# A four-layer attention and GLU kernel: the order of the first chunk's set-up, a shared scratch tile, masks by one minimum, and a planner with ranks

## The chip, the cores and the metric

The kernel runs on one core of one Trainium2 chip. A core has a matrix engine (TensorE, PE), a vector engine (VectorE, DVE), a scalar engine (ScalarE, ACT), a general engine (GpSimd, POOL) and a sync engine (SyncE, SP) that issues DMA transfers here. Each engine works through its own list of instructions in order and waits on semaphores that other engines or transfers raise. The metric is the device time of one execution, in microseconds; lower is better.

## The reference

Four layers run over x of shape [1, 2048, 576]: attention, GLU, attention, GLU, all with the same two sets of weights. Each layer adds its result to its input after a layer norm without scale or offset:

```python
x = x + _A_ref(_layernorm(x), A_wqkv, A_wo)
x = x + _B_ref(_layernorm(x), B_w_gate, B_w_up, B_w_down)
...
```

Attention has 32 heads of 18 values. A position attends to itself and to the seven positions 2, 4, ..., 14 steps before it; positions before the start are masked:

```python
idx = pos[:, None] - off[None, :]        # off = 0, 2, ..., 14
logits = jnp.where(idx >= 0, einsum("bhsd,bhswd->bhsw", q, kg) * scale, -1e9)
o = jnp.einsum("bhsw,bhswd->bhsd", softmax(logits), vg)
...  # then o @ wo
```

The GLU computes ((x @ w_gate) * (x @ w_up)) @ w_down with 4608 hidden values and no activation function. Inputs and output are bf16.

## The kernel before

**Tiling.** The 2048 positions are cut into chunks of 256; the first four chunks of the first attention layer have 128. `seq` lists 18 chunks, numbered j from 0: six of the first attention layer (0 to 3 with 128 positions), then four of the second over the same first 1024 positions, then four and four over the other 1024. For each chunk the kernel does attention and then the GLU (`attention(j, ...)`, `glu(j, ...)`). All weights stay in SBUF except w_down, of which 288 KB pieces (`wd`, seven buffers) are loaded again for each chunk.

**Attention of a chunk.** `head` (L356) does the layer norm: statistics on DVE, two small steps on ACT for 1/sigma (`rstd`), one on DVE (`nmr`), the normalisation on ACT (`xn`), a transpose on PE for the first five chunks (L395, by transposing DMA later), and the copy out of PSUM on ACT (L400). `project` (L446, matmuls in L456) computes q, k and v with heads along partitions; the weights are copied once into another column order for that (`wqkv` from `wraw`, L310 DVE, L312 POOL, L314 ACT). DVE multiplies q by two shifted k's at a time (four products, L554); PE sums them over the values of a head with a 0/1 matrix (`Esel`, L569); softmax runs on DVE and ACT (L590 to L602); PE spreads the weights over the partitions (L612); DVE multiplies them with the eight shifted v's (L642), PE (chunk 0, L646 and L647) or DVE (L656) adds these up; PE multiplies by wo (L669), in four pieces for 256 positions and two for 128, and DVE adds the residual (L675). A second `head` prepares the input of the GLU, `xnT_B`.

**GLU of a chunk.** Three phases, each of gate and up matmuls (L720; L731 for the last 64 rows of the contraction), a copy of gate on ACT (L742), a product on DVE (L743), the down matmuls (L759, L760) and an addition to x on DVE (L772).

**The order.** Nothing is ordered by hand. Every step is an `op` with an engine, an estimated cost, the keys it reads and writes, a priority and a `margin` (a time by which it is planned later than its inputs allow). `Plan.run` (L74) simulates the engines with these estimates: it takes the op that can start first, by (time, priority, index), and emits its instructions in that order. Its one exception: ops marked `due` (the GLU's L742 and L743) may take the place of another op of their engine:

```python
if not o.due and o.eng in urgent and urgent[o.eng][0][0] < best[0][0] + o.cost - SLACK[o.eng]:
    best = urgent[o.eng]
```

What an engine does in hardware is this order; the times are those of the hardware. PE, DVE and ACT so hold the work of several chunks mixed: the GLU of one chunk, the attention of the next ones.

**The start.** SP issues, in this order: x of the first 128 positions, the raw wqkv weights in six transfers (four of 128 rows with all 1728 columns, and twice the last 64 rows), x of three more chunks' positions, x for chunk 4, wo (six), then the GLU's weights in six slices with the first `wd` pieces between them. Each transfer uses one of eight semaphores in turn, so that it is issued once the eighth transfer before it has landed. In chunk 0 (`fast`) the projection runs over the five row blocks of the weights as they arrive, and each row block's matmuls wait for q, k and v columns alike. `wraw` lives in a pool of its own that is given back (`swap`) when all copies are done; the product buffers, `Lt` and `ab` are taken from the same place after that. Masks of chunk 0 are seven memsets on the logits in PSUM (L590).

Of the kernel before, what the change touches and what calls it, by code (L numbers as in the profile page):

```python
# [7 lines left out]
FP32 = mybir.dt.float32  # L8
BF16 = mybir.dt.bfloat16
# [6 lines left out]
class Op:  # L16
    __slots__ = ("eng", "cost", "fn", "deps", "order", "succ", "n", "prio", "idx", "hold", "free",
                 "lat", "margin", "ready", "end", "nbytes", "use", "pair", "need", "due", "late")
# [3 lines left out]
SLACK = {"DVE": 500, "ACT": 300}  # L22


class Plan:
# [6 lines left out]
    def __init__(self):  # L32
        self.ops = []
        self.wr = {}
        self.rd = {}

    def op(self, eng, cost, fn, r=(), w=(), prio=1, after=None, hold=None, free=None, margin=0, nbytes=0, use=None,
           pair=None, need=None, due=False, late=0):
        o = Op()
        o.due, o.late = due, late  # L40
# [33 lines left out]
    def run(self, slots):  # L74
# [5 lines left out]
        while cand:  # L80
            best = None
            urgent = {}
            for o in cand:
# [60 lines left out]
def kernel(  # L144
# [56 lines left out]
    Bsel = sb("Bsel", [P, 4, 4, 32])  # L201
    xf_all = sb("xf", [P, NXS, NST, D], FP32)
# [26 lines left out]
    startup_pool = tc.tile_pool(name="startup", bufs=1)  # L229
    sp = startup_pool.__enter__()  # L230
    wraw = sp.tile([P, KT, 3 * D], BF16, name="wraw")
    late = {}
# [35 lines left out]
    def load_x(t0, nst, tmp=False):  # L268
# [3 lines left out]
           nbytes=P * nst * D * 2, prio=0 if t0 == 0 else 1.2 if t0 < 2 else 1.5)  # L272

    def setup_a():
# [6 lines left out]
        for k in range(KF):  # L281
            op("SP", 500, dma(wraw[:, k, :], A_wqkv[k * P:(k + 1) * P, :]), w=[f"wraw{k}"], nbytes=P * 3 * D * 2, prio=1)
        for r_ in (0, TL):
            op("SP", 500, dma(wraw[r_:r_ + TL, KF, :], A_wqkv[KF * P:D, :]), w=[f"wrawt{r_}"], nbytes=TL * 3 * D * 2, prio=1)

    def setup_b():
# [11 lines left out]
        for k in range(KT):  # L298
            for t3 in (0, 1, 2, 3):
                if t3 < 3:  # L300
                    src = wraw[:, k, t3 * D:(t3 + 1) * D].rearrange("p (h d) -> p d h", h=H)[:, 0:16, :]
                    dst = wqkv[:, k, t3 * 512:(t3 + 1) * 512].rearrange("p (d h) -> p d h", h=H)
                    cost = (525, 1000)
                else:
                    src = wraw[:, k, :].rearrange("p (t h d) -> p t d h", t=3, h=H)[:, :, 16:18, :]
                    dst = wqkv[:, k, 3 * 512:3 * D].rearrange("p (t d h) -> p t d h", t=3, h=H)
                    cost = (230, 440)
                rk = [f"wraw{k}"] if k < KF else ["wrawt0", f"wrawt{TL}"]
                if t3 == 0 or t3 == 3:
                    op("DVE", cost[0], lambda dst=dst, src=src: nc.vector.tensor_copy(dst, src), r=rk, w=[f"wq{t3}_{k}"], prio=2)  # L310
                elif t3 == 2:
                    op("POOL", 1000, lambda dst=dst, src=src: nc.gpsimd.tensor_copy(dst, src), r=rk, w=[f"wq{t3}_{k}"], prio=2)  # L312
                else:
                    op("ACT", cost[1], lambda dst=dst, src=src: nc.scalar.copy(dst, src), r=rk, w=[f"wq{t3}_{k}"], prio=2)  # L314
# [9 lines left out]
        op("POOL", 3200, mk_sel, w=["sel"], prio=3)  # L324

        def swap():
            startup_pool.__exit__(None, None, None)
            rot = ctx.enter_context(tc.tile_pool(name="rot", bufs=1))
            late["prod"] = [rot.tile([P, 2, KT, CH], BF16, name=f"prod{i}") for i in range(2)]
# [533 lines left out]
```

## Time and profile before

| | us |
|---|---|
| median of 3 runs | 1087.86 |
| lowest, highest | 1087.48, 1089.80 |
| profiled execution, its own time | 1089.71 |
| profiled execution, span from first to last instruction | 1087.9 |
| PE busy | 1054.1 |
| DVE busy | 777.7 |
| ACT busy | 353.8 |
| POOL busy | 13.4 |
| first matmul of the GLU (L720) | 43.57 |

The profile is of one execution. Times within it count from the first instruction. "PE ... <- DVE ..." in the list of waits means that PE stood idle and that an instruction of DVE ended the wait; then come total us, how often, and the longest. In the timeline a row has start, us, engine, line, operation, output and inputs, shape, how many, and in brackets the idle time ahead and what ended it. In the table of stretches each engine's busy us stand with its instruction count (PE, weight loads, DVE, ACT, POOL), then the granted clock of PE (1.00 is full), the DMA share and GB/s.

### The profile page before, as it was taken

The page shows a single profiled execution, that of the slowest core. Times are in us where ns is not written, and L with a number is a line of the kernel's source. Part 1 is how long each engine was busy: PE and PEld are TensorE (multiplying, and loading weights), DVE is VectorE, ACT ScalarE, POOL GpSimd, SP SyncE. Part 2 cuts the span into 40 slices and gives each one's busy share as a digit, 9 for nine tenths or more (in the row PEclk, how much of TensorE's full clock was granted, in tenths as well). Part 3 has the DMA queues.
Part 4 walks back from the last instruction along what each step waited for, and adds up shares of the span by engine and source line. Part 5 has one row for each costly group of instructions (what it writes and reads, how often), then busy time and mean ns, then how long its engine had stood idle before and what let it go on. Part 6 is the DMA issues. An engine that isn't in the chain of part 4 may idle for free.

```text
span 1087.9 us, 25318 instructions
## 1 busy us (share of the span) xinstructions
PE 1054.1 (97%) x10758; PEld 792.0 (73%) x10824; DVE 777.7 (71%) x1388; ACT 353.8 (33%) x704; POOL 13.4 (1%) x30
## 2 busy tenths in 40 slices
PE   5889999999999999999999999999999999999998
PEld 4767877777777766777777677777677677777775
DVE  7678888898898968898897633775787767523232
ACT  6633354331435333133333212325133242212121
POOL 4000000000000000000000000000000000000000
PEclk8989999999999999999999999999999999999999
DMA  9944645534426152344443434233442334342422
GB/s 273 327 150 141 200 144 154 147 83 118 113 79 168 20 160 79 115 107 118 111 134 91 126 94 130 82 101 91 130 104 79 113 85 149 78 142 66 143 67 66
DMA packets 145905, 132.75 MB, mean 122 GB/s; under 512 B 42048, under 2 KB 145152, under 8 KB 145792
## 3 DMA queue, kind: packets, MB, share of 16 engines
q1 hardware_dynamic: 145792, 131.13, 42.9%
q8 instruction: 84, 1.38, 0.5%
q14 instruction: 29, 0.24, 0.1%
HBM read 118.51 MB, written 4.06 MB: 113 GB/s over the span
## 4 chain that ended last, share of the span: by engine, by line
PE 85%; DVE 11%; DMA 1%; issue 1%; ACT 0%; SPq 0%; DVEq 0%; ACTq 0%
PE pu L720 22%; PE pg L720 22%; PE pg L759 10%; PE pu L759 8%; PE pg L731 6%; PE pg L456 5%; PE pu L456 4%; PE acct L760 3%; PE pa L669 3%; DVE oT L656 3%; DVE prod L642 3%; DVE h L743 1%; DVE prod L554 1%; DMA wraw<-in_A_wqkv_dram 1%; PE pa L569 1%
## 5 line engine op out<-in xcount | busy, mean ns | idle before, releaser
L742 ACT CAST g_sb<-pg 128x512 bf16<-128x512 f32 x288 | 159.1, 587 | 460.1 <-PE pu L731 342.1
L720 PE MATMUL pg<-xnT_B,wg 128*128 128x256 bf16 (+1 forms) x2592 | 299.8, 261 | 0.8 <-ACT xnT_B L400 0.8
L720 PE MATMUL pu<-xnT_B,wu 128*128 128x256 bf16 (+1 forms) x2592 | 300.2, 261 | 0.0
L743 DVE TENSOR_TENSOR h<-pu,g_sb 128x512 bf16<-128x512 f32 x288 | 192.8, 685 | 130.8 <-ACT g_sb L742 79.3
L720 PEld LDWEIGHTS <-wu 128*128 128x128 bf16 x2592 | 224.0, 98 | 39.5 <-issue 16.7
L720 PEld LDWEIGHTS <-wg 128*128 128x128 bf16 x2592 | 228.2, 98 | 30.2 <-issue 1.5
L760 PE MATMUL acct<-wd,h 128*128 128x64 bf16 x1152 | 222.5, 193 | 3.4
L759 PE MATMUL pg<-wd,h 128*128 128x512 bf16 x593 | 213.0, 383 | 0.0
L759 PEld LDWEIGHTS <-h 128*128 128x128 bf16 x1152 | 113.0, 98 | 129.7 <-issue 1.7
L759 PE MATMUL pu<-wd,h 128*128 128x512 bf16 x493 | 187.3, 380 | 0.4 <-DVE h L743 0.4
L456 PEld LDWEIGHTS <-wqkv 128*128 128x128 bf16 (+1 forms) x1260 | 99.4, 100 | 25.7 <-issue 13.3
L760 PEld LDWEIGHTS <-h 128*128 128x128 bf16 x1152 | 113.1, 98 | 1.5 <-issue 0.4
L554 DVE TENSOR_TENSOR prod<-qT,kv 128x2560 bf16<-128x2560 bf16 (+1 forms) x68 | 90.0, 1326 | 27.9 <-ACT kv L498 26.8
L656 DVE TENSOR_TENSOR oT<-oT,prod 128x1280 bf16<-128x1280 bf16 (+1 forms) x119 | 90.9, 764 | 3.2
L642 DVE TENSOR_TENSOR prod<-kv,ab 128x1280 bf16<-128x1280 bf16 (+1 forms) x120 | 88.0, 736 | 2.1 <-PE pg L647 1.9
L456 PE MATMUL pg<-xnT_A,wqkv 128*128 128x256 bf16 (+3 forms) x650 | 80.6, 266 | 1.6 <-POOL wqkv L312 0.8
L772 DVE TENSOR_TENSOR xf<-pg,xf 128x512 f32<-128x512 f32 (+1 forms) x54 | 36.6, 678 | 60.1 <-PE pg L759 60.1
L731 PE MATMUL pu<-xnT_B,wgu_t 64*128 64x256 bf16 (+1 forms) x648 | 79.4, 259 | 0.0
L731 PE MATMUL pg<-xnT_B,wgu_t 64*128 64x256 bf16 (+1 forms) x648 | 79.4, 259 | 0.0
L456 PE MATMUL pu<-xnT_A,wqkv 128*128 128x256 bf16 (+3 forms) x610 | 78.2, 268 | 0.0
L731 PEld LDWEIGHTS <-wgu_t 64*128 64x128 bf16 x1296 | 50.3, 94 | 23.3 <-issue 18.3
L669 PE MATMUL pa<-wo_p,oT 128*128 128x288 bf16 x310 | 48.2, 286 | 6.2 <-DVE oT L656 4.5
(98 smaller groups left out, 629.6 us busy)
## 6 DMA issues: line engine op xcount, KB each, us to landing
wd<-in_B_w_down_dram SPq DMA_DIRECT2D x324, 288.0 KB, 3.5
ab<-a_dram SPq DMA_DIRECT2D x52, 128.0 KB, 2.7
wg<-in_B_w_gate_dram SPq DMA_DIRECT2D x6, 768.0 KB, 9.8
wu<-in_B_w_up_dram SPq DMA_DIRECT2D x6, 768.0 KB, 10.8
out_dram<-xf SPq DMA_DIRECT2D x8, 288.0 KB, 2.7
wraw<-in_A_wqkv_dram SPq DMA_DIRECT2D x4, 432.0 KB, 5.4
xb<-in_A_x_dram SPq DMA_DIRECT2D x6, 288.0 KB, 3.0
a_dram<-s SPq DMA_DIRECT2D x13, 128.0 KB, 1.9
```

Of the source, the lines that this page charges most:

```text
L456: nc.tensor.matmul(bank(p_, u)[0:m, e * n:(e + 1) * n], lhsT=wqkv[r_, k, w0:w0 + m], rhs=xnT_A[r_, k, c0:c0 + n], start=start, stop=stop, ...
L554: nc.vector.tensor_tensor(late["prod"][p_ % 2][:, :, :, 0:n], q2, k2, op=ALU.mult)
L642: nc.vector.tensor_tensor(js(dst), js(vT[:, :, o0:o0 + n]), abw, op=ALU.mult)
L656: op("DVE", 70 + 2.63 * n, lambda i_=i_: nc.vector.tensor_tensor(oT[:, :, 0:n], oT[:, :, 0:n], late["prod"][i_ % 2][:, 0, :, 0:n], op=ALU. ...
L669: nc.tensor.matmul(b()[:, 0:HD], lhsT=oT[:, t, i * P:(i + 1) * P], rhs=wo_p[:, t, hh * HD:(hh + 1) * HD], start=(t == 0), stop=(t == KT - 1))
L720: nc.tensor.matmul(pt[:, e * n:(e + 1) * n], lhsT=w_[:, k, ft * P:(ft + 1) * P], rhs=xT[:, k, 0:n], start=(first and k == 0 and e == 0), s ...
L731: nc.tensor.matmul(ps[:, e * n:(e + 1) * n], lhsT=wgu_t[r_, ft * P:(ft + 1) * P], rhs=xT[r_, KF, 0:n], start=(first and e == 0), stop=not ...
L742: op("ACT", 490, lambda: nc.scalar.copy(g_sb[gs][:, 0:ul], pg[use["slot"]][:, 0:ul]), r=[f"wg_{j}_{u}"], w=[f"g{gs}"], prio=0, due=True)
L743: op("DVE", 605, lambda: nc.vector.tensor_tensor(hb[hs][:, 0:ul], pu[use["slot"]][:, 0:ul], g_sb[gs][:, 0:ul], op=ALU.mult), r=[f"wu_{j}_{ ...
L759: nc.tensor.matmul((pg, pu)[i][use["slot"]][:], lhsT=lhs, rhs=wt[:, e % 2, 0:512], start=first, stop=fin)
L760: nc.tensor.matmul(acct[:, i * TL:(i + 1) * TL], lhsT=lhs, rhs=wt[:, e % 2, 512:D], start=(first and i == 0), stop=fin, skip_group_check=True)
L772: op("DVE", 600, lambda i=i, dst=dst: nc.vector.tensor_tensor(dst[:, 0:512], (pg, pu)[i][use["slot"]][:], xs_f[:, i0 + i, 0:512], op=ALU.add),
```

## The change

*Loads.* x of the first 256 positions is loaded first. The raw weights come in twelve transfers: first the q and k columns of all rows (`wrawa`), then the v columns (`wrawb`). Then follow the other x tiles, wo and the GLU's weights as before.

*Scratch tile.* `wrawa`, `wrawb`, the two product buffers, the four `s1` buffers, `Lt` and `ab` are slices of one tile `scr`; the pool and its `swap` are gone, and two empty ops order the reuse.

*Weight copies.* The q columns and the last values of q and k are copied on DVE, the k columns on DVE and ACT in turn, all of v on POOL. POOL also writes a table `cap` with eight memsets.

*Projection of chunk 0.* All q and k matmuls stand first, by row block, then all v matmuls; the copies out of PSUM follow each part on its own.

*Masks.* One minimum with `cap`.

*Statistics of chunk 0's GLU input.* They are taken in two halves, each when its half of the residual is there (`halves`).

*Planner.* `due` becomes a rank: -1 for the due ops, 0 for set-up and chunk 0's attention, the chunk's number for later attentions, 60 for the GLU. An op of rank 0 or below may take the place of an op of a higher rank on DVE, ACT and PE, within the bounds `IDLE` and `SLACK`. The projections of chunks 2 and 3 are ordered after chunk 0's last output projection (`late["wo"]`). From chunk 6 on the margin is 1200 ns in place of 500. The rate that the plan assumes for SP's transfers is 320 in place of 250 bytes per ns, and the cost of chunk 0's sums on PE is half.

```diff
+SLACK = {"DVE": 500, "ACT": 300, "PE": 0, "POOL": 0, "SP": 0}
+IDLE = (2000, 300)
+LOOK = {"DVE": 1, "ACT": 1, "PE": 1, "POOL": 0, "SP": -9}
...
-                if o.due and (o.eng not in urgent or key < urgent[o.eng][0]):
-                    urgent[o.eng] = (key, o)
+                urgent.setdefault(o.eng, []).append((key, o))
             o = best[1]
-            if not o.due and o.eng in urgent and urgent[o.eng][0][0] < best[0][0] + o.cost - SLACK[o.eng]:
-                best = urgent[o.eng]
+            if o.rank > 0:
+                end = best[0][0] + o.cost
+                ahead = [(c[1].rank, c[0], c[1]) for c in urgent[o.eng] if c[1].rank < o.rank and c[1].rank < LOOK[o.eng]
+                         and c[0][0] < end - SLACK[o.eng] * (c[1].rank < 0)
+                         and c[0][0] < best[0][0] + IDLE[min(max(c[1].rank, 0), 1)]]
+                if ahead:
+                    best = min(ahead, key=lambda c: c[:2])[1:]
...
-                dma[o.eng] = max(dma[o.eng], o.end) + o.nbytes / (250.0 if o.eng == "SP" else 200.0)
+                dma[o.eng] = max(dma[o.eng], o.end) + o.nbytes / (320.0 if o.eng == "SP" else 200.0)
...
-    wraw = sp.tile([P, KT, 3 * D], BF16, name="wraw")
+    scr = sb("scr", [P, 10368])
+    wrawa = scr[:, 0:KT * 2 * D].rearrange("p (k n) -> p k n", k=KT)
+    wrawb = scr[:, KT * 2 * D:KT * 3 * D].rearrange("p (k n) -> p k n", k=KT)
+    late = {"prod": [scr[:, 2560 * i:2560 * (i + 1)].rearrange("p (a k s) -> p a k s", a=2, k=KT) for i in range(2)],
+            "s1": [scr[:, o:o + 512].rearrange("p (a s) -> p a s", a=2) for o in (5120, 5760, 6272, 6784)],
+            "a_c": scr[:, 6784:7296],
+            "Lt": scr[:, 7296:8320].bitcast(FP32),
+            "ab": scr[:, 8320:10368].rearrange("p (j s) -> p j s", j=4)}
...
-        for k in range(KF):
-            op("SP", 500, dma(wraw[:, k, :], A_wqkv[k * P:(k + 1) * P, :]), w=[f"wraw{k}"], nbytes=P * 3 * D * 2, prio=1)
+        for c, wr, c0, c1 in (("a", wrawa, 0, 2 * D), ("b", wrawb, 2 * D, 3 * D)):
+            for k in range(KF):
+                op("SP", 470, dma(wr[:, k, :], A_wqkv[k * P:(k + 1) * P, c0:c1]), w=[f"wraw{c}{k}"], nbytes=P * (c1 - c0) * 2, prio=1)
...
+            perm("DVE", 530, f"wq0_{k}", 0, ra)
+            perm("DVE", 180, f"wq3_{k}", 3, ra)
+            if k % 2:
+                perm("DVE", 530, f"wq1_{k}", 1, ra)
+            else:
+                perm("ACT", 1000, f"wq1_{k}", 1, ra)
+            perm("POOL", 1250, f"wq2_{k}", 2, rb)
+            perm("POOL", 250, f"wq4_{k}", 4, rb)
...
+        def mk_cap():
+            nc.gpsimd.memset(cap[:], 3e38)
+            for i_ in range(W):
+                if wlist[i_] > 0:
+                    nc.gpsimd.memset(cap[:, i_, 0:DIL * wlist[i_]], -1e9)
...
-        prio, mg = (1, 0) if fast else (3, 500)
+        prio, mg = (1, 0) if fast else (3, 500 if j < 6 else 1200)
...
+                for part in (0, 1):
+                    u, parts, ts = (ua, au + bu[4:5], (0, 1, 3)) if part == 0 else (ub, bu[:4] + bu[5:], (2, 4))
...
                 o1 = op("PE", len(au) * KF * n * 0.428, lambda: full(ua, au, True, False), r=xk + wk, w=[ka], prio=0, margin=400,
-                        pair=(ua, ub))
+                        pair=(ua, ub), after=late["wo"] if 2 <= j < 4 else None)
...
             if t0 == 0:
-                for i_ in range(W):
-                    if wlist[i_] > 0:
-                        nc.vector.memset(pav[0:32, i_, 0:DIL * wlist[i_]], -1e9)
+                nc.vector.tensor_tensor(pav[0:32, :, 0:HALO], pav[0:32, :, 0:HALO], cap[:], op=ALU.min)
...
-        head(lambda i: xs_f[:, i0 + i, :], fk, nst, xnT_B[j % NXB], f"xB{j % NXB}_", prio - 1, 1, on_pe, mg)
+        head(lambda i: xs_f[:, i0 + i, :], fk, nst, xnT_B[j % NXB], f"xB{j % NXB}_", prio - 1, 1, on_pe, mg, halves=fast)
...
+        pl.rank = min(j, 50)
         attention(j, l, t0, nst)
+        pl.rank = 60
```

More of the change, by code (lines that the diff above doesn't have):

```diff
@@ L17 @@
     __slots__ = ("eng", "cost", "fn", "deps", "order", "succ", "n", "prio", "idx", "hold", "free",
-                 "lat", "margin", "ready", "end", "nbytes", "use", "pair", "need", "due", "late")
+                 "lat", "margin", "ready", "end", "nbytes", "use", "pair", "need", "rank", "late")
 POOLQ = False
-SLACK = {"DVE": 500, "ACT": 300}
+SLACK = {"DVE": 500, "ACT": 300, "PE": 0, "POOL": 0, "SP": 0}
+IDLE = (2000, 300)
+LOOK = {"DVE": 1, "ACT": 1, "PE": 1, "POOL": 0, "SP": -9}
 class Plan:
@@ L33, in __init__ @@
         self.ops = []
+        self.rank = 0
         self.wr = {}
@@ L489, in project @@
             for u, key, evs in ((ua, ka, ea), (ub, kb, eb)):
[L490 to L492 removed]
+                for cost, fn, w_, eng, *early in evs:
+                    op("DVE" if fast and eng else "ACT", cost, lambda fn=fn, u=u, eng=eng: fn(u, fast and eng),
+                       r=[ka if early else key], w=w_, prio=min(prio, 1), free="unit", use=u)
         def cp(on_dve, dst, src):
```

114 lines of the change are left out of this document (62 added, 52 removed).

## The prediction

> **What bounds the kernel now.** I read the page first, then the waits of PE, then a table of stretches, then the timeline around each hole.
>
> ```profile
> span 1087.9 us, 25318 instructions
> ...
> PE 1054.1 (97%) x10758; PEld 792.0 (73%) x10824; DVE 777.7 (71%) x1388; ACT 353.8 (33%) x704; POOL 13.4 (1%) x30
> ...
> PE   5889999999999999999999999999999999999998
> ```
>
> PE is busy for 97% of the span, so only 33.8 us of holes, and matmuls run at a reduced clock, can be won. The slices put most of the holes in the first 54 us. The waits of PE say who ended them:
>
> ```profile
> PE pu L395 <- ACT xn L382: 6.6, 1, 6.6
> PE pa L669 <- DVE oT L656: 4.5, 5, 2.0
> PE pa L395 <- ACT xn L382: 4.2, 2, 3.7
> PE acct L569 <- DMA wo_p<-in_A_wo_dram: 2.9, 1, 2.9
> ```
>
> The first is the start. The fourth is named after a DMA, but its matmuls read the first product of chunk 0, which DVE wrote at 16.72: it is the wait for the first products. The 3.7 us in the third is one hole. Stretches of the span (PE busy, then the other engines, then the granted clock):
>
> ```profile
> 0.00:14.65 14.65, 6.46 (x76) 5.59 (x77) 8.75 (x19) 8.76 (x11) 13.44 (x30) 1.00 0.90 246
> 14.65:36.70 22.05, 15.71 (x261) 12.70 (x259) 16.35 (x48) 14.31 (x35) 0.00 (x0) 0.85 1.04 316
> ...
> 69.10:73.57 4.47, 0.69 (x6) 0.26 (x5) 4.33 (x12) 1.36 (x3) 0.00 (x0) 0.89 0.61 181
> 73.57:79.42 5.85, 5.85 (x46) 3.05 (x47) 2.77 (x8) 1.11 (x2) 0.00 (x0) 0.50 0.46 121
> ...
> 400.00:420.00 20.00, 17.90 (x146) 12.06 (x146) 19.23 (x31) 4.99 (x11) 0.00 (x0) 0.91 0.34 104
> ```
>
> So there are two places: the start up to 36.7 us, and a hole at 69.7 us after which PE is granted half its clock for 5.85 us more. The timeline, in three pieces (DVE, POOL, PE):
>
> ```profile
> 8.70 0.62 DVE L310 COPY wqkv<-wraw 128x512 bf16<-128x512 bf16 x1 [1.58 <-DMA wraw<-in_A_wqkv_dram]
> 10.34 1.49 DVE L310 COPY wqkv<-wraw 128x512 bf16<-128x512 bf16 x1 [0.61 <-DMA wraw<-in_A_wqkv_dram]
> ...
> 22.78 0.84 DVE L590 MEMSET acct<- 32x2 f32 x7
> ...
> 32.10 0.89 DVE L642 TENSOR_TENSOR prod<-kv,ab 128x640 bf16<-128x640 bf16 x2 [1.57 <-PE pg L647]
> ...
> 7.71 6.55 POOL L312 COPY wqkv<-wraw 128x512 bf16<-128x512 bf16 x5
> ...
> 36.70 0.79 PE L669 MATMUL acct<-wo_p,oT 128*128 128x288 bf16 x5 [0.89 <-ACT oT L659]
> ...
> 73.57 0.61 PE L395 MATMUL pa<-ident,xn 128*128 128x128 bf16 x4 [3.73 <-ACT xn L382]
> ```
>
> **The change part by part: the start.** I follow chunk 0 to its output projection (36.70 before).
>
> *Loads.* 14 transfers (two of x, 12 of weights) replace seven, at some 0.48 us of SP each (six in 3.16 us). The last q and k row is the eighth issue, at about 4.1 us. Ahead of its end lie 2 x 144 + 4 x 288 + 2 x 144 = 1728 KB. Before, 1440 KB had arrived at 8.70 and 1872 KB at 10.34 (the two DVE releases above), so it lands at about 9.8; the last raw piece released ACT at 12.23. The bytes up to the fourth x tile are the same as before, so the loads behind (wo, the GLU weights) keep their places but for the seven extra issues, 7 x 0.48 = 3.4 us of SP at most; the first GLU matmul at 43.57 stands some 20 us behind the landing of its weights (issue 14.07 plus the page's 9.8), which covers that even if it comes 4 us sooner.
>
> *Copies and projection.* After 9.8 come one ACT copy (1.1) or two short DVE copies (0.55 + 0.2), then the q and k tails on PE: done by 11.3. Before, the tails ended at 14.65, because PE waited for POOL's last v copy (7.71 + 6.55 = 14.26). Gain 3.3. Evacuation to first product took 2.07 (14.65 to 16.72): the first product is due at 13.4.
>
> *Products.* Four took 4.1 (16.72 to 20.82) with three small instructions and a statistics group between them; now they stand in a row, 4 x 0.78 = 3.1: end at 16.5, gain 4.3.
>
> *Masks.* Seven memsets, 0.84 us, become one minimum over 32x8x14 in PSUM. No row shows it: between 0.12 (one of the memsets) and 0.42 (the 128x256 reduction of the same bank); I take 0.25, nearer the memset, as 112 elements are. Two statistics groups (2.0 us) still precede it. Reduction at 18.7 instead of 23.66, gain 4.9. From there to the first v product nothing changes (4.96 us): 23.7 instead of 28.62.
>
> *v products.* From 28.62 to the output projection it took 8.1 us, of which DVE waited 1.57 + 0.31 + 0.99 for gathers on PE that stood behind chunk 2's projection. In the built order of the changed kernel's PE instructions that projection stands behind the output projection (it is ordered after it), so 5.2 us: output projection at 28.9, gain 7.8. But PE still has to do the 70 matmuls (37.93 to 41.67 for chunk 3's, 3.74 us), so the net is **4.1 us**.
>
> *POOL.* The masks' eight memsets (about 1 us) come before the v copies; v's first piece lands at about 10.3 and POOL was free at 7.71, so they are hidden. Five copies of 1.1 and five short ones (0.2 to 0.5, as 192 columns took DVE 0.49) end at about 17.3. PE takes its v matmuls between the product sums, and everything of chunk 1 queues behind the last of them; chunk 1's projection began at 21.25 before, so there are 3 us of room.
>
> *Collision.* New is that the four products now run while POOL copies. The two DVE rows above are the same copy: 0.62 alone, 1.49 while POOL's copy held from 10.24. DVE statistics at 13.62 beside POOL took 0.45 as always. A two-input product beside a POOL copy is in no row. Ends: nothing, like the statistics, and 4 x 0.9 = 3.6, like the copy. I take two collisions, **2.0 us** lost (about the middle; both kinds of row are equally near).
>
> The Trainium skill, SBUF — State Buffer, section "SBUF: two separate sides", says that GpSimd and VectorE take turns on one pair of ports as an exclusive lock, and counts among VectorE's lock takers an operation with two SBUF inputs against a GpSimd operation that reads SBUF. By that rule all four products are exposed; the loss would be 3.6 in place of 2.0. The copies agree with the lock (0.62 against 1.49); for products no run here shows it.
>
> Net of the start: 4.1 - 2.0 = 2.1. Half clock in 14.65:36.70 (0.85) is taken to stay as it was; it could go or double, 1.9 us either way (16 matmuls of chunk 1's projection took 1.82 us in place of 0.89).
>
> **The hole at 69.7.** Chunk 1's second output projection ended at 69.1, and PE had 0.6 us of down matmuls ahead of the transposes that need residual, statistics, rstd, normalisation: 69.10 to 73.57, 4.47 us. In the changed kernel's order, 48 GLU matmuls, 24 tails and 16 more stand there: 2.78 + 0.78 + 0.90 = 4.46 us by the spacing of the same groups in this trace. So the hole of 3.9 closes to about 0.2. With it goes the half clock: from 73.57 to 79.42 PE did what takes 3.0 us at full clock (512-column matmuls lasted 0.61 against 0.38), 2.8 lost. Gain **6.5**.
>
> **The rest.** The wider margin from chunk 6 on and the loads' rate in the plan only reorder. After 100 us PE waited 6.7 us (6.1 for output projections) and lost 1.7 at half clock near 410. Ends: all but the small ones gone (-5), or a wait of 0.72 added in each of the 12 chunks from 6 on (+8.6). I take nothing. The minimum, split statistics and the sharing of the tile are within chunk 0 and counted.
>
> Sum: 2.1 + 6.5 = 8.6. The profiled execution took 1089.71 us (span 1087.9), 1.85 over the median of the runs; 1089.71 - 8.6 = 1081.1 there, 1087.86 - 8.6 = **1079.2** as median.
>
> **The rivals.** (a) Products blocked fully: 1087.86 - (4.1 - 3.6) - 6.5 = 1080.9. For: the copy's 1.49. Against: the statistics' 0.45. (The Trainium skill's lock, above, is this case.) (b) The hole moves: precedence is given to chunk 0 alone, and chunk 1's DVE chain can run later than 4.47 or the next chunk can meet the same; then only the start is won, 1085.8. Against: DVE has as much to do there as before. (c) The later waits shrink as well: 1079.2 - 5 = 1074.2. For: 1200 ns in place of 500 puts other matmuls ahead of each output projection. (d) Slower: the same margin makes output projections late. Residual, statistics and the GLU's input of each chunk hang on them; if every GLU from chunk 6 on starts late, 12 x 0.72 eats the 8.6, and 0.9 us each gives 1090. For: PE has no slack to catch up. Against: five waits there, 2.0 the longest, are for DVE, so PE is early, not late.
>
> **How the numbers follow.** Forecast, start and hole both won: 0.50, 1077 to 1082. (a) 0.17; (b) 0.13; (c) 0.11; (d) 0.06; no gain at all 0.03. The range 1074 to 1085.5 leaves out (d), no gain, half of (b) and a third of (c), about 0.19. Faster by over 0.2% (2.2 us, about what a measurement tells from no change): 0.90; within 0.03; slower 0.07.
>
> **What would show it.** First product near 13.4 and four of 0.8 each (longer: collision); output projection of chunk 0 at 29 to 31; no wait over 1 us for chunk 1's transposes at 60 to 70 us and clock 1.00 there; PE waits after 100 us still near 6.7. Wrong, if POOL's copies end after 20 us and hold PE, or if PE's waits for output projections after 100 us exceed 10 us.

## The result, and the profile after

The changed kernel takes 1083.69 us in the median of 14 runs (1081.33 to 1087.24), the kernel before 1088.63 in the median of 14 (1086.39 to 1090.75): a ratio of 0.9959, 95% interval 0.9945 to 0.9974, or 4.9 us less. The forecast was 8.6 us less. Beside the experiments below the changed kernel was measured four more times, each time together with the kernel before: 1081.94, 1082.34, 1082.78 and 1082.11 us, ratios 0.9938, 0.9938, 0.9934 and 0.9948, which is 5.8 to 7.0 us less. Six of the 14 executions of the first measurement were above 1085 us, none of the 22 later ones. Their mean granted clocks, 0.993 to 0.996, overlap those of the other eight, 0.994 to 0.997; what made those six longer, no run shows.

The profiled execution of the changed kernel (1081.68 us, span 1079.6) is 8.3 us of span shorter than that of the kernel before (1087.9). That is nearly the sum of the forecast, but the terms of the sum are others than forecast: the hole was won as forecast, the start won nothing, and the later chunks won what the start did not. How this comes about is the subject of what follows.

The page of the changed kernel: the span, the busy time and share of the engines, and PE's slices of the span in tenths.

```profile
span 1079.6 us, 25395 instructions
...
PE 1056.3 (98%) x10824; PEld 792.3 (73%) x10824; DVE 781.2 (72%) x1378; ACT 351.9 (33%) x703; POOL 18.4 (2%) x43
...
PE   5999999999999999999999999999999999999998
```

PE's busy time hardly changed (1054.1 before, with 10758 of the 10824 matmuls on record); the slices from the second on are full. The waits of PE in the changed kernel (us in total, times, longest):

```profile
PE pu L418 <- ACT xn L405: 7.6, 1, 7.6
PE acct L611 <- DVE scr L596: 2.2, 2, 1.5
PE pa L709 <- DVE oT L696: 1.6, 2, 1.3
...
PE pa L709 <- DVE xf L715: 1.4, 3, 0.7
```

The waits for output projections (bank pa, ended by DVE) are 3.0 us in place of 6.1, which were the 4.5 us of a line that the prediction shows and the 1.6 of this one:

```profile
PE pa L669 <- DVE xf L675: 1.6, 2, 0.9
```

The 3.7 us ahead of chunk 1's transposes are gone. The first wait, of the start, has become a microsecond longer. A table of stretches of the changed kernel (PE busy, the other engines, then the granted clock):

```profile
12.62:16.04 3.42, 1.60 (x25) 1.15 (x24) 2.78 (x5) 1.78 (x5) 3.42 (x6) 1.00 1.00 242
16.04:26.28 10.24, 9.08 (x150) 7.47 (x150) 8.70 (x21) 4.13 (x13) 3.58 (x3) 0.50 1.04 329
...
60.00:80.00 20.00, 19.98 (x320) 16.95 (x317) 15.63 (x38) 9.46 (x20) 0.00 (x0) 1.00 0.39 119
400.00:420.00 20.00, 18.42 (x171) 14.46 (x169) 19.52 (x34) 5.37 (x13) 0.00 (x0) 1.00 0.18 56
```

From 60 to 80 us PE is busy for 19.98 of 20 at full clock: the hole and the half clock behind it are both gone, and so is the half clock near 410 us (0.91 before). At the start, however, half clock lasts 10.24 us, three steps of 3.41; before it was two (18.0 to 24.8). The timeline of the start, in pieces of DVE, POOL and PE (start, duration, what was waited for in brackets):

```profile
14.37 1.02 DVE L399 SCALAR_TENSOR_TENSOR nmr<-mv,rstd 128x1 f32<-128x1 f32 x1
15.32 4.15 DVE L596 TENSOR_TENSOR scr<-qT,kv 128x1280 bf16<-128x1280 bf16 x4
...
21.70 0.42 DVE L631 TENSOR_REDUCE mx<-acct 128x32 f32<-128x256 f32 x1
...
24.44 0.42 DVE L642 TENSOR_TENSOR scr<-scr,zs 128x256 bf16<-128x256 f32 x1
...
28.90 4.01 DVE L682 TENSOR_TENSOR scr<-kv,scr 128x640 bf16<-128x640 bf16 x8
...
9.91 9.71 POOL L322 COPY wqkv<-scr 128x512 bf16<-128x512 bf16 x10 [0.37 <-DMA scr<-in_A_wqkv_dram]
...
16.18 0.46 PE L611 MATMUL acct<-scr,Esel 128*32 128x64 bf16 x20 [1.46 <-DVE scr L596]
...
21.56 1.86 PE L479 MATMUL pg<-xnT_A,wqkv 128*128 128x128 bf16 x16 [0.25 <-ACT xnT_A L423]
...
27.48 0.38 PE L652 MATMUL pu<-scr,Bsel 128*128 128x256 bf16 x2
...
34.06 0.79 PE L709 MATMUL acct<-wo_p,oT 128*128 128x288 bf16 x5 [0.63 <-ACT oT L699]
...
43.95 1.07 PE L762 MATMUL pg<-xnT_B,wg 128*128 128x128 bf16 x16
```

The normalisation's small instruction (`nmr`, on one column) takes 1.02 us beside POOL's copies and the four products 4.15. The attention weights are ready when DVE's product of 24.44 ends, at 24.86, but the four matmuls that spread them stand on PE behind chunk 1's projection, which runs from 21.56 to 27.48, at half clock up to 26.28. So the first v product waits until 28.90. The same places in the kernel before (DVE, then PE):

```profile
23.66 0.42 DVE L591 TENSOR_REDUCE mx<-acct 128x32 f32<-128x256 f32 x1
...
28.62 1.91 DVE L642 TENSOR_TENSOR prod<-kv,ab 128x640 bf16<-128x640 bf16 x4
...
21.25 1.89 PE L456 MATMUL pg<-xnT_A,wqkv 128*128 128x128 bf16 x16
```

The first GLU matmul, the last line of the changed kernel's timeline, is the measure for the start. PE has the same matmuls to do before it in both kernels (an estimate of 22.7 us, by the spacing of each form in the trace of before), so what the start won or lost shows in that one time: 43.57 before, 43.95 in the changed kernel, and 44.38, 44.70, 44.25 and 43.66 in its later profiles. The start lost 0.1 to 1.1 us; the forecast had it at 43.57 - 2.1 = 41.5.

### The profile page after: what moved, and what is told of

It reads as the page before. It is cut to its first block, busy times and chain, and to the rows that moved or that the text cites. A ratio compares the mean times of both kernels' runs of the same rounds, so it can differ in the third digit from the quotient of the medians.

```text
span 1079.6 us, 25395 instructions
## 1 busy us (share of the span) xinstructions
PE 1056.3 (98%) x10824; PEld 792.3 (73%) x10824; DVE 781.2 (72%) x1378; ACT 351.9 (33%) x703; POOL 18.4 (2%) x43
## 4 chain that ended last, share of the span: by engine, by line
PE 78%; DVE 15%; DMA 3%; issue 1%; SPq 1%; ACT 0%; DVEq 0%; ACTq 0%
PE pu L762 20%; PE pg L762 20%; PE pg L801 11%; PE pu L801 8%; PE pg L773 6%; PE pg L479 4%; PE pa L709 3%; PE pu L479 3%; DVE scr L682 3%; PE acct L802 3%; DVE oT L696 2%; DVE scr L596 2%; DVE h L785 2%; DMA scr<-a_dram 1%; DMA a_dram<-scr 1%
## 5 line engine op out<-in xcount | busy, mean ns | idle before, releaser
L801 PE MATMUL pg<-wd,h 128*128 128x512 bf16 x648 | 228.7, 380 | 0.0
L801 PE MATMUL pu<-wd,h 128*128 128x512 bf16 x504 | 191.5, 380 | 1.5 <-DVE h L785 1.4
L596 DVE TENSOR_TENSOR scr<-qT,kv 128x2560 bf16<-128x2560 bf16 (+1 forms) x68 | 90.9, 1338 | 26.4 <-ACT kv L533 26.3
L696 DVE TENSOR_TENSOR oT<-oT,scr 128x1280 bf16<-128x1280 bf16 (+1 forms) x119 | 90.9, 764 | 3.3
L682 DVE TENSOR_TENSOR scr<-kv,scr 128x1280 bf16<-128x1280 bf16 (+1 forms) x120 | 88.3, 737 | 0.3
```

The lines of the kernel that those rows point to most:

```text
L596: nc.vector.tensor_tensor(late["prod"][p_ % 2][:, :, :, 0:n], q2, k2, op=ALU.mult)
L682: nc.vector.tensor_tensor(js(dst), js(vT[:, :, o0:o0 + n]), abw, op=ALU.mult)
L696: op("DVE", 70 + 2.63 * n, lambda i_=i_: nc.vector.tensor_tensor(oT[:, :, 0:n], oT[:, :, 0:n], late["prod"][i_ % 2][:, 0, :, 0:n], op=ALU. ...
L801: nc.tensor.matmul((pg, pu)[i][use["slot"]][:], lhsT=lhs, rhs=wt[:, e % 2, 0:512], start=first, stop=fin)
```

## The experiments

### Which half of the change brings the gain

The changed start with the planner of before:

```
-            if o.rank > 0: ...                        (precedence by rank)
+            if not o.due and o.eng in urgent and ...  (the rule of before)
-        prio, mg = (1, 0) if fast else (3, 500 if j < 6 else 1200)
+        prio, mg = (1, 0) if fast else (3, 500)
-                        pair=(ua, ub), after=late["wo"] if 2 <= j < 4 else None)
+                        pair=(ua, ub))
```

> The changed start (loads, copies, minimum, split statistics) with the planner's rule, margin and order of the kernel before. Theory A: the start gains nothing, because its half clock grew from 6.8 to 10.2 us and the collisions cost more than was taken; all that was won is the hole near 70 us. Then this kernel is within 1.5 us of the kernel before, and chunk 1's transposes near 70 us still wait over 2 us. Rival B: an earlier chunk 0 is what lets chunk 1 come in time; then 6 to 8 us faster than before, and no such wait.

Measured (e1): 1088.02 us against 1088.95, ratio 0.9995 (0.9981 to 1.0008).

The start of before with the changed planner (the same lines the other way round, in the kernel before):

> The start of the kernel before with the changed planner's rule, the margin of 1200 from chunk 6 and chunks 2 and 3 projected behind chunk 0's output projection. Theory A: the hole is closed by the order of the matmuls (some 4.4 us of them between chunk 1's output projection and its transposes), so 5 to 8 us faster than before: near 1081 to 1083. Rival B: without the earlier start the hole stays, and this kernel is within 1.5 us of the kernel before.

Measured (e2): 1081.52 us against 1088.95, ratio 0.9934 (0.9916 to 0.9953). One line of the table of stretches of each, the start alone first:

```profile
60.00:80.00 20.00, 14.30 (x183) 10.46 (x182) 15.43 (x38) 5.30 (x10) 0.00 (x0) 0.83 0.44 133
```

```profile
60.00:80.00 20.00, 19.93 (x318) 17.01 (x318) 15.64 (x38) 9.46 (x20) 0.00 (x0) 1.00 0.41 128
```

With the start alone PE is idle for 5.7 of these 20 us, with the planner alone for 0.07. Theory A holds: the order of PE's matmuls closes the hole, whatever the start, and the new start by itself brings nothing that can be told from zero. The planner alone is as fast as the whole change (0.9934 and 0.9938, measured side by side).

### The margin, to which the forecast gave the worth of zero

```
-        prio, mg = (1, 0) if fast else (3, 500 if j < 6 else 1200)
+        prio, mg = (1, 0) if fast else (3, 500)
```

> The changed kernel with the margin of 500 for all chunks, as before. Theory G (the wider margin only reorders, its worth is 0): within 1 us of the changed kernel, PE's waits after 100 us as there. Rival H (the margin is what shortened the later waits and took the half clock near 410 us away): 2 to 4 us slower than the changed kernel, PE busy near 296.3 us in 100 to 400, as in the kernel before, in place of 298.6.

Measured (e7): 1087.24 us (ratio 0.9986, 0.9974 to 0.9998), where the changed kernel beside it took 1082.34 (0.9938). The waits of PE after 100 us, with the margin of 500 first, then of the changed kernel on the same chip:

```profile
PE pa L709 <- DVE oT L696: 5.2, 7, 1.5
PE pa L709 <- DVE xf L715: 1.9, 5, 0.7
```

```profile
PE pa L709 <- DVE oT L696: 1.8, 2, 1.6
PE pa L709 <- DVE xf L715: 1.0, 4, 0.3
```

Rival H holds. Without the margin PE waits 7.1 us for output projections, with it 2.8; the difference, 4.3 us, is most of the 4.9 us between the two medians. The hole stayed closed (PE busy for 19.92 us from 60 to 80). So a kernel that had won the 6.5 us of the hole is only 1.7 us faster than before: the start took 1.3 (first GLU matmul at 44.87 against 43.57), and the rest was given back after 100 us. By the first weight load of each chunk's GLU, its profile is 4.8 us ahead of that of before at chunk 1 and 2.3 at the last chunk, where the five profiles of the changed kernel are 4.9 to 6.0 us ahead at chunk 1 and 6.4 to 8.8 at the last. That what was given back are waits for output projections that PE now reaches too early is shown in part only: in the list of waits they grew by 1.0 us, from 6.1 to 7.1, in one profile each.

The margin in the kernel before, with nothing else changed (`(3, 500)` becomes `(3, 500 if j < 6 else 1200)`):

> The kernel before with nothing but the margin of 1200 from chunk 6 on. Theory H (the margin shortens the later waits for output projections, whatever the start): PE's waits for output projections after 100 us fall from 7.5 to 4 us or less, the hole near 70 us stays, and the kernel is 2 to 4 us faster than before. Rival G (the margin is worth something only with the changed rule of precedence): within 1 us of before.

Measured (e9): 1087.29 us against 1089.43, ratio 0.9984 (0.9972 to 0.9995): 2.1 us faster, at the low end of H. PE's waits for output projections after 100 us fell from 6.1 to 2.9, and the hole is still there (PE busy for 16.25 us from 60 to 80). The margin is worth 2.1 us there and 4.9 behind a closed hole.

### What the start lost: half clock

Matmuls of 512 columns on the identity into the bank pa, ahead of and between those of chunk 0:

```
+    def fill(n):
+        for _ in range(n):
+            nc.tensor.matmul(pa[:, 0:512], lhsT=ident[:], rhs=ident[:].unsqueeze(1).to_broadcast([P, 4, P]), ...)
 def tr(...):
+                if first: fill(16)
     ...transposes...
+                if first: fill(3)
 ...
                                 full(ua, au, k == 0, False, [k]); mm(ub, bu[4], ...)
+                                fill(1)
 (behind the tails of q and k)
+                                fill(5)
 (behind each product sum but the last)
+                                fill(1)
```

> The changed kernel with idle matmuls of 512 columns on the identity, into a bank of PSUM that nothing else uses yet: 16 ahead of the first transposes, then 3, four times 1, 5 and three times 1 in the gaps of chunk 0's projection and of its product sums, so that PE is busy from 1.4 us on. Theory A (half clock is what the start loses): the clock is 1.00 from about 8 us on, the tails of q and k end near 12.2 in place of 13.3, chunk 1's projection ahead of the spread takes 3.5 in place of 5.8 us, and the whole is 2 to 5 us faster than the changed kernel. Rival E (DVE's chain and its collisions set the start, whatever the clock): within 1 us of the changed kernel, or slower by the added matmuls' 0.2 to 1 us.

Measured (e4): 1079.97 us against 1088.95, ratio 0.9923 (0.9901 to 0.9945); the changed kernel beside it 1081.94 (0.9938). Once more:

> The changed kernel with the added matmuls, POOL's copies as they were: 1.5 to 2.5 us faster than the changed kernel if half clock is a cost of its own; within 1 us of it if the first look at it was chance.

Measured (e15): 1081.31 us, ratio 0.9935 (0.9920 to 0.9949); the changed kernel beside it 1082.11 (0.9948). The gain in the whole, 2.0 and 0.8 us, lies within the intervals, so the whole does not decide between A and E. The start does: the first GLU matmul is at 42.23 and 40.76, against 43.66 to 44.70, and the first v product follows the reduction after 5.75 and 4.96 us, against 6.21 to 7.40 in the five profiles of the changed kernel (7.20 in the first). The first of the two runs still had one step of 3.4 us at half clock, the second none; in the second chunk 1's projection takes 3.78 us (20.51 to 24.29) in place of 5.92. From the timeline of the second (DVE and POOL):

```profile
15.50 3.01 DVE L609 TENSOR_TENSOR scr<-qT,kv 128x1280 bf16<-128x1280 bf16 x4
...
10.29 9.66 POOL L327 COPY wqkv<-scr 128x512 bf16<-128x512 bf16 x10 [0.71 <-DMA scr<-in_A_wqkv_dram]
```

Here the four products ran beside POOL's copies in 3.01 us. Of the ten copies the short one at 15.50 took 3.17 us, where the others like it took 0.29 to 0.35: it waited for the products, and not the products for the copies. In the changed kernel's first profile the short copy at 15.31 took 2.44 beside three products of 0.81, and the fourth product then took 1.75 beside a long copy of 1.09. Which of the two waits differs from one execution to the next.

### What the start lost: DVE beside POOL

The copies of v's weights left out (zeros in their place):

```
-            perm("POOL", 1250, f"wq2_{k}", 2, rb)
-            perm("POOL", 250, f"wq4_{k}", 4, rb)
+            op("POOL", 1250, lambda: None, r=rb, w=[f"wq2_{k}"], prio=2)
+            op("POOL", 250, lambda: None, r=rb, w=[f"wq4_{k}"], prio=2)
```

> The changed kernel without POOL's ten copies of v's weights; the columns are filled with zeros by DVE in its first idle microsecond, so v is left out of the computation. Every order is the changed kernel's. Theory F (the collisions cost the start what was won): the normalisation's small instruction at 14.4 takes 0.17 in place of 1.02, the four products take 0.8 each, the reduction comes 2 to 3 us earlier (19 to 19.7 in place of 21.7), and the whole is 1 to 3 us faster than the changed kernel. Rival A (half clock is what the start loses): the reduction comes earlier too, but the spread still waits behind chunk 1's projection at half clock until 26 to 27.5, and the time stays within 1 us of the changed kernel's.

Measured (e5): 1079.35 us (ratio 0.9915, 0.9902 to 0.9928), 3.0 us under the changed kernel beside it (1082.34). The small instruction takes 0.14, the four products 3.03, the reduction comes at 20.50. So theory F has the time right. But the first v product is still at 27.46, 6.96 us behind the reduction, as rival A has it: chunk 1's projection runs from 20.65 to 26.04, at half clock up to 24.05. The first GLU matmul is at 42.45.

> Both: without POOL's copies of v's weights (v left out of the computation), and with the added matmuls that keep PE busy from 1.4 us on. If collisions and half clock together are what the sum had wrong at the start, the output projection of chunk 0 comes near the 28.9 us that were forecast (28.5 to 30.5; 34.1 in the changed kernel, 32.3 with the added matmuls alone), and the time is 3 to 5 us under the changed kernel's. If something else holds the start, over 31 and less than 3 us.

Measured (e6): 1078.06 us (ratio 0.9900, 0.9887 to 0.9912). From its timeline (DVE, then PE):

```profile
14.21 3.03 DVE L610 TENSOR_TENSOR scr<-qT,kv 128x1280 bf16<-128x1280 bf16 x4
...
24.24 0.89 DVE L697 TENSOR_TENSOR scr<-kv,scr 128x640 bf16<-128x640 bf16 x2
...
29.33 0.79 PE L724 MATMUL acct<-wo_p,oT 128*128 128x288 bf16 x5 [0.63 <-DMA wd<-in_B_w_down_dram]
```

With both losses taken away the reduction is at 19.48, the first v product 4.76 us behind it, the output projection at 29.33 (28.9 forecast) and the first GLU matmul at 39.22, where the forecast without collisions was 43.57 - 4.1 = 39.5. The time is 4.3 us under the changed kernel's. On chunk 0's path the forecast without collisions comes out within 0.8 us at each of these places; what it left out or mis-sized is what these two runs took away. (In both, v is not computed.)

### The same with v computed

First all five large copies on ACT:

```
-            perm("POOL", 1250, f"wq2_{k}", 2, rb)
+            perm("ACT", 1000, f"wq2_{k}", 2, rb)     (the last three ordered behind q's eviction)
```

> The changed kernel with the five large copies of v's weights on ACT (two of them ahead of q's eviction, three behind it) in place of POOL; the short ones stay on POOL. Theory F (POOL's copies hold DVE up): as without the copies, the four products take 0.8 each and the kernel is 2 to 3 us faster than the changed one. Rival: ACT, which now does 5.5 us more between 11 and 18 us, delays q's eviction or chunk 1's normalisation and gives it back: within 1 us of the changed kernel.

Measured (e10): 1084.30 us (ratio 0.9955, 0.9939 to 0.9971); the changed kernel beside it 1082.78 (0.9934). The products took 0.8 each, as F has it, but the kernel is 1.5 us slower and not faster, which is worse than the rival's 1 us. One cause is the rival's: the normalisation of chunk 1's tile, at 15.47 in the changed kernel, came at 18.98 on ACT, behind the three copies. Another it did not name: the plan, which expects q's eviction later when ACT has more to do, put a group of statistics of a later tile ahead of the products (1.0 us, from 13.54). PE then waited 1.7 us for a copy of v's weights, 1.4 for that tile and 1.8 for the attention weights. With the added matmuls it was no better:

> The same with the matmuls that keep PE busy from 1.4 us on. If the two costs of the start (POOL's copies beside DVE, PE at half clock) add, 4 to 5 us faster than the changed kernel, near 1077.5 to 1078.5, with the output projection of chunk 0 near 29.5; if they are one and the same, as the run before this.

Measured (e11): 1084.61 us (ratio 0.9956, 0.9938 to 0.9973), output projection at 30.92, and the clock at half for one step all the same. These two runs do not separate the costs, since they moved other work as well: their first GLU matmul comes at 36.44 and 36.87, before two projections that the other kernels do ahead of it.

Then two copies on ACT and three on POOL, ACT's two counted at nothing in the plan so that DVE's order up to the products stays:

```
-            perm("POOL", 1250, f"wq2_{k}", 2, rb)
+            perm("ACT" if k < 2 else "POOL", 0 if k < 2 else 1250, f"wq2_{k}", 2, rb)
```

> The changed kernel with the first two large copies of v's weights on ACT, in its idle time before q's eviction, and three on POOL, which is then done before the products; the plan counts ACT's two at nothing, so that DVE's order up to the products stays the changed kernel's. Theory F (POOL's copies beside DVE cost the start 2 to 3 us): POOL ends near 15, the four products take 0.8 each, 1.5 to 3 us faster than the changed kernel, with v computed. Rival: what the runs without v showed came from v's matmuls not having to wait, not from the products; then within 1 us of the changed kernel.

> v's copies split between ACT and POOL, without added matmuls, once more, on the same chip: ratio to the kernel before 0.990 to 0.993 as at first, and 0.5 to 2 us slower than with the added matmuls.

Measured (e13, e18): 1079.45 us (ratio 0.9914, 0.9901 to 0.9927; the changed kernel beside it 1082.11, 0.9948, 0.9936 to 0.9960), and in the second measurement 1077.54 us (0.9902, 0.9884 to 0.9920). No wait of PE in the changed kernel's five profiles ends with one of POOL's copies, which speaks against the rival, that v's matmuls had to wait for them. The timeline of the second (DVE, then POOL), and under it a stretch of it:

```profile
14.71 3.19 DVE L597 TENSOR_TENSOR scr<-qT,kv 128x1280 bf16<-128x1280 bf16 x4
...
11.13 3.88 POOL L323 COPY wqkv<-scr 128x512 bf16<-128x512 bf16 x6 [0.21 <-DMA scr<-in_A_wqkv_dram]
```

```profile
16.00:26.00 10.00, 7.75 (x167) 6.27 (x157) 9.46 (x25) 6.30 (x17) 0.00 (x0) 1.00 1.07 311
```

POOL is done at 15.0, the products take 3.19, and the clock stays at 1.00 with no matmul added. The output projection is at 29.45 and the first GLU matmul at 39.35 (31.25 and 41.14 in the first of the two runs, in which half clock lasted for one step of 3.4 us). Not all of this is the collisions: the plan, which sees v's copies done sooner, also moved one group of statistics (1.0 us) from ahead of the reduction to behind it, and the spread ahead of the last 1.35 us of chunk 1's projection. What the collisions cost by themselves is read from e5, whose orders are the changed kernel's. This kernel computes everything and beats both kernels.

With the added matmuls on top:

> The same with the matmuls that keep PE busy from 1.4 us on. If collisions and half clock are two costs that add: 3.5 to 5 us faster than the changed kernel, 1077.5 to 1079, output projection of chunk 0 at 29 to 31 us. If the added matmuls stand in the way of the earlier products: no faster than the run before this.

Measured (e14): 1077.84 us (ratio 0.9907, 0.9893 to 0.9922). The added matmuls behind its third product sum overwrote part of chunk 1's transposes, so it was run with only the first of the groups behind the product sums:

> The run with v's copies split between ACT and POOL and with the added matmuls (e14), but of the matmuls behind the product sums only the first. In e14 those behind the third sum fell behind chunk 1's transposes and overwrote them in their bank, so its input of chunk 1 was altered; its time is that of the same instructions. If the two costs of the start add: 1077 to 1079 again, and the output projection of chunk 0 at 29 to 31 us; if e14 was fast only because something was left out: as e13 alone, 1079.5 or more.

Measured (e17): 1078.27 us (ratio 0.9907, 0.9892 to 0.9922), beside 1077.54 without the added matmuls. With the added matmuls the output projection is at 30.92 (e14) and 29.86 (e17). The times are those forecast for two gains that add, but the run without added matmuls was as fast: beside e13 they went with 1.6 us less, beside e18 with 0.7 us more, both within the intervals. That the two gains add is therefore not shown here; e18, which had no half clock, left the added matmuls none to take away. Without any copies, in the changed kernel's order (e5), half clock still lasted two steps; so the collisions are not its only cause.

### The changed kernel again

> The changed kernel once more, unaltered. Its executions lay in two groups, 1081.3 to 1082.1 and 1083.6 to 1087.2. Theory C: the groups differ by waits of PE in the middle of the kernel (the mean granted clock is 0.993 to 0.997 in both), so a profile of an execution above 1085 shows 3 to 5 us more of PE's waits, and no more half clock. Rival D: they differ by half clock; then such a profile shows 6 to 10 us more of it.

> The changed kernel unaltered, beside the three others. In the first measurement half of its executions took 1083.6 to 1087.2 and the others 1081.3 to 1082.1; in the second all took 1080.1 to 1082.7. If the upper group belongs to the phase of the clock's windows, it comes again in about half of the executions here; if it belonged to the chip of the first measurement, all lie under 1083 again.

> The changed kernel beside the three others, for the differences above: 1081 to 1083 as in the two later measurements, or two groups as in the first.

> The changed kernel beside the three others, for the differences above: 1081 to 1083.

Measured (e3, e8, e12, e16): medians 1081.94, 1082.34, 1082.78 and 1082.11, all executions from 1079.03 to 1084.65. No execution above 1085 came again, so neither C nor D could be tried. The start of kernels in which PE has an estimated 22.5 to 22.7 us of matmuls ahead of the first GLU matmul (added ones not counted), times of chunk 0 in us. The three later profiles of the changed kernel (e8, e12, e16) lie between 43.66 and 44.70 in the last column:

| kernel | four products | reduction | first v product | output projection | first GLU |
|---|---|---|---|---|---|
| before | 16.72 to 20.82 | 23.66 | 28.62 | 36.70 | 43.57 |
| forecast | 13.4 to 16.5 + 2.0 | 18.7 + 2.0 | 23.7 + 2.0 | 28.9 + 2.0 | 41.5 |
| changed | 15.32, 4.15 | 21.70 | 28.90 | 34.06 | 43.95 |
| changed, e3 | 15.12, 4.93 | 22.29 | 29.32 | 34.49 | 44.38 |
| planner alone | 16.88, 3.03 | 21.76 | 27.79 | 32.87 | 42.77 |
| filled, e4 | 15.01, 4.19 | 21.43 | 27.18 | 32.34 | 42.23 |
| filled, e15 | 15.50, 3.01 | 20.75 | 25.71 | 30.87 | 40.76 |
| no v copies | 15.23, 3.03 | 20.50 | 27.46 | 32.54 | 42.45 |
| no v copies, filled | 14.21, 3.03 | 19.48 | 24.24 | 29.33 | 39.22 |
| v split, e13 | 15.97, 3.03 | 20.31 | 25.96 | 31.25 | 41.14 |
| v split, e18 | 14.71, 3.19 | 19.20 | 24.17 | 29.45 | 39.35 |

The row of the planner alone holds a surprise: with the old loads and copies the first GLU matmul is at 42.77 in its one profile, earlier than in any of the five of the whole change. To the new planner the new loads and copies, as they stand in the changed kernel, are no gain.

## Why the prediction was right and wrong

**The hole (6.5 us): right.** Chunk 1's transposes no longer wait, the half clock behind them is gone, and the planner alone shows it without the start. Between 40 and 100 us PE loses 0.6 us to idle gaps and slow matmuls, in place of 7.3 (an estimate, summed over the spacings of its matmuls): 6.7 won. Rival (b) fell.

**The rest (0): wrong, and this is the term that saved the sum.** The forecast gave the margin no worth, between -5 and +8.6. PE's waits for output projections after 100 us fell from 6.1 to 3.0, and the half clock near 410 us (1.7) went: close to rival (c), to which 0.11 was given. The runs with the margin alone and without it show that it is the margin (2.1 and 4.9 us). What the forecast did not work out is what is late next where a stall goes: when the hole closes, PE reaches later output projections earlier while DVE does not. With the margin of 500 those waits rose to 7.1; that this is the whole of what was given back there is not shown. Rival (d), late output projections by the margin, fell.

**The start (+2.1): wrong; it lost 0.1 to 1.1.** By its steps:

*Loads, 9.8 for the last piece of q and k:* right, it landed at 9.59. *Copies and projection done by 11.3:* wrong. The pieces are copied one after another on DVE, from 5.67 to 11.87 without a wait, so the landing was not what set the pace; and PE did each piece of nine matmuls in 0.96 us (10.16 to 11.12), 107 ns a matmul, where the same matmuls took 56 ns behind 13.3. The column of the granted clock shows 1.00 there, as no change is on record before 12.62. The tails ended near 13.3, and the first product was at 15.32. Of the 2.0 us between, 0.85 was the collision of the small instruction, so that the evacuation without it took 1.1 in place of the 2.07 that were forecast.

*Collisions, 2.0:* about right in size. The small instruction lost 0.85 and the products 1.1 (4.15 against 3.03), 1.9 in all; in e3 the products lost 1.9. Rival (a), all four blocked, fell: one lost 0.9 in the first profile, and two lost as much in e3. The minimum took 0.27 (0.25 forecast). At the reduction the changed kernel is 1.0 us behind the forecast with collisions, 21.70 against 20.7.

The Trainium skill, SBUF — State Buffer, section "SBUF: two separate sides", says that whichever of the two engines starts first holds the pair of ports for its whole instruction. The runs agree, and show both outcomes: a product of 1.75 beside a copy of 1.09, and a short copy of 3.17, where its like take 0.29, beside four products of 0.81. Statistics, which read one tile, took 0.81 beside POOL as they do alone.

*Reduction to the first v product, "nothing changes (4.96 us)":* this is the step that failed. It took 7.20, and with the 1.0 us at the reduction it makes up the 3.2 us by which the output projection missed its forecast, 34.06 against 30.9. The four spreading matmuls stand on PE behind chunk 1's projection, in both kernels. Before, that projection began at 21.25, ahead of the reduction at 23.66; in the changed kernel it began no earlier, 21.56, since it follows the product sums and the transposes on PE, and with half clock up to 26.28 it takes 5.9 us. So the earlier reduction (21.70) gained nothing, and PE set the time. Where the projection runs at full clock, in 3.78 us, the step is as short as forecast: 4.96 beside POOL's copies (e15) and 4.76 without them. Without the copies but with half clock it stays at 6.96 (e5).

*"Half clock of the start stays as it was" (1.9 either way):* wrong in what it touches. The term counted only PE's slower work, and the half clock lay on the path of DVE's chain as well: the q and k matmuls up to 12.62, and chunk 1's projection ahead of the spread. That it went from two steps of 3.41 us to three in four of the five profiles (10.24 us in a row in the first) comes on top. The remaining steps, v products to output projection in 5.2 (5.16 measured) and the 3.74 us of chunk 2's projection behind it, held.

**What was to be seen.** First product near 13.4 with 0.8 each: no, 15.3 and 4.15 for four. Output projection at 29 to 31: no, 34.06, but 29.33 and 29.45 in the runs without the two losses. No wait over 1 us at 60 to 70 us: yes. PE's waits after 100 us near 6.7: no, 4.9. POOL's copies ended at 19.62, and at 18.27 to 20.21 in the four later profiles, where after 20 us would have told of a hold; no wait of PE in any of them ends with one of these copies.

So a size near 8.6 us came out in the profiled execution by luck: two errors cancelled. By an estimate summed over the spacings of PE's matmuls, the start to 40 us lost 0.9, the hole won 6.7 and the rest 2.7: 8.5 by the end of the last matmul. The weight loads say the same: the first of chunk 1's GLU is 5.7 us earlier than before, the last of all 8.5. In the medians of five measurements it was 4.9 to 7.0, as the profiled execution of before, 1089.71 us, lay above its median and that of the changed kernel, 1081.68, below.

## What to carry to other kernels

When a stall is closed early in a kernel whose engines all run near full, work out what the engine meets next: here the kernel was 4.9 us slower with the margin left at 500 than with 1200, most of it in waits for output projections of later chunks. A chain on one engine that waits for another engine's queue is not shortened by starting it sooner, if what stands ahead in that queue is not moved as well: without v's copies the reduction came at 20.50, and the first v product still at 27.46. Copies on POOL beside two-input work on DVE can be worth moving to an engine that is idle just then: with two of the five moved to ACT the changed kernel was 2.7 us faster (1082.11 to 1079.45), in part by what the plan then reordered, while all five on ACT made it 1.5 slower.

## What the hardware showed that was not expected

Half clock came without any long gap. In the stretch ahead of the fall, 12.62 to 16.04, PE was busy for 1.60 of 3.42 us, and its longest wait there, of 1.46, ended at 16.18; then three steps followed at 0.50, although PE was busy for 9.08 of those 10.24 us. The Trainium skill, TensorE: Matmul & The Clock Gate, section "HAM oscillation — how this bites in real kernels", has the rule that no idle gap of PE should be longer than about 3.4 us. By that rule the clock would have stayed; the measurement decides, and here a stretch that was half idle in short pieces was enough. It is not always: in the step of 3.41 us from 11.80 in e18 and from 12.67 in e15, PE was busy for 1.90 and 1.85 us and full clock stayed, while in e5, from 13.81, it was busy for 2.13 and the clock fell (steps counted from the first change on record). So PE's busy time in a step does not by itself say whether the clock falls. The steps also begin at another time in each execution (12.62 here, 11.80 in e18, 13.81 in e5), so that one profile does not say how often a kernel meets half clock.

An instruction of DVE on one column, 0.14 us alone, took 0.30 to 1.08 us in the nine profiles in which it fell beside a copy on POOL, and ended 0.01 to 0.02 us behind that copy each time: what it lost to the collision was set by what was left of the other engine's instruction, not by its own length.
